# An attention and gated MLP kernel on one core: GpSimd clears, staggered prologue deadlines, and another split of exponentials between ScalarE and VectorE

## Chip, cores and metric

One core of a Trainium2 chip. The metric is the device time of one execution in microseconds (us), lower is better. Every run quoted here was in the fast state, with a granted TensorE clock of about 0.99.

## The reference

```python
xn = layernorm(x)                        # x: 1 x 2048 x 640, bf16
qkv = xn @ wqkv                          # 32 heads of 20
p = softmax(q k^T / sqrt(20));  s = (p v) @ wo
h  = gelu(layernorm(xn) @ w1)            # the side branch
x1 = xn + shift(h) @ w2                  # four column groups shifted by 1 or 2 rows
h2 = gelu(layernorm(x1) @ w3) @ w4       # 640 -> 1536 -> 640
out = x + s * silu(x1 + h2)
```

Softmax needs 32 x 2048 x 2048 exponentials. They are the bulk of the work.

## The kernel before

Heads are worked on four at a time: eight quads (0 to 7), each with four groups of 512 queries. A group has score tiles of 128 x 1024 in PSUM. ScalarE turns one into exponentials in one instruction (an "exp" below). Some tiles are taken in blocks by VectorE instead, which builds the exponential's bits with integer operations in several pieces; such a block takes two exps off ScalarE. The numbers in `ND` say how many blocks each group of each quad has.

The order of every engine is fixed when the kernel is built: the kernel carries a list scheduler with its own model of how long each operation takes, and `DUE` shifts the deadlines of the tasks. DMAs are issued from SyncE. `dlat` shifts the model's estimate of when a transfer lands.

```python
self.DUE = dict(k0=164.5, ..., v0=-37.7, v0s=0.02, ..., u7=-16.2, s7=52.2)
self.POOLN = [6, 7, 9, 12, 14]          # tiles normalised on GpSimd
self.TRA = [9, 11, 15, 19]              # transposes evicted by ScalarE
self.LAST = [[[4, 2], [7, 1]], [[6, 1]]]  # VectorE units in the two halves of the last group
self.ND = ([1,2,4,3], [2,3,3,4], [3,4,2,2], [3,2,4,4], [3,2,4,3], [4,3,4,3], [4,4,3,2], [4,4,3,0])
# ... cut ...
ms = pl.schedule(verbose=True)
```

The exponential, two PSUM banks (`hs`) in, one buffer of `PT` out:

```python
def exp_act(self, hs, sa):
    self.T("act", c_act(1024),
           lambda e: e.activation(self.PT[:, hp.slot, :], self.psum[:, 512*hs.slot:512*hs.slot+1024], AF.Exp, scale=cfg.scale),
           reads=[sa], writes=[pa], name=f"exp{self.step}", due=self.at(self.nact + 1), acq=("PT", hp), rel=hs)
```

After each group the sums go to DRAM and back, and their reciprocals once more, to be broadcast over partitions (cut to the second trip):

```python
T("sp", C_SP, lambda e: e.dma_start(dr[ob]..., RZ[:, ob, :]), reads=[A("RZ", ob)], writes=[("dr", ob)],
  is_dma=True, nbytes=8192, name=f"r0{quad}_{qc}", stream="r0", dlat=-840.0)
T("sp", C_SP, lambda e: e.dma_start(RB[:, :], bass.AP(dr.tensor, ...)), reads=[("dr", ob)], writes=[A("RB")],
  is_dma=True, nbytes=128 * 2048, name=f"r1{quad}_{qc}", stream="r1", dlat=3600.0)
```

The last group of quad 7 is worked in two halves of 256 queries; `LAST` gives the places and numbers of score tiles that VectorE takes there (each by itself, one exp fewer).

```python
for unit in at.get(x, []):
    for m, kx in enumerate(unit):
        hs, sa = scores(kx, "d")         # takes a score slot, like ScalarE's tiles
        T("dve", c_dve(1024), ...)       # first piece: reads PSUM, frees the slot
# ... cut: pieces from SBUF, then the sums on PE
```

Of the kernel before, what the change touches and what calls it, by code (L numbers as in the profile page):

```python
# [610 lines left out]
class Cfg:  # L611
# [5 lines left out]
    def __init__(self, S=2048, D=640, H=32, F=1536):  # L617
        self.S, self.D, self.H, self.F = S, D, H, F
        self.DH = D // H
        assert self.DH == 20 and D % 128 == 0 and F % 128 == 0 and S % 512 == 0  # L620
        self.NT = S // 128
        self.NQC = S // 512
        self.KC = D // 128
        self.FC = F // 128
        self.NQUAD = H // 4
        self.QW = 4 * self.DH
        self.scale = self.DH ** -0.5
        self.OFFSET = 60.0
        self.T0 = 38000.0
        self.STEP = 960.0  # L630
        self.DUE = dict(
            k0=164.5, k1=-174.5, k2=-113.6, k3=-166.6, k4=-173.8, v0=-37.7, v0s=0.02, v1=3.5, v1s=-17.41, w1=870.8,
            w1s=6.09, g1=108.7, x1=247.5, x1s=-10.34, wo=4.2, st=212.5, g3_0=333.3, g3_2=544.8, si_0=498.9, si_2=652.8,
            sis=10.98, u0=6.1, s0=-19.0, u1=82.8, s1=39.0, u2=-14.0, s2=-6.0, u3=-32.6, s3=24.8, u4=-8.0, s4=-2.3,
            u5=-17.0, s5=-15.1, u6=-44.4, s6=75.8, u7=-16.2, s7=52.2)
        self.BLK = [(2, 3), (6, 7), (10, 11), (14, 15)]
        self.RESERVE = 1000.0
        self.POOLN = [6, 7, 9, 12, 14]
        self.HPE = 0.0
        self.HDVE = 0.0  # L640
        self.THIRD = False
        self.FALL = False
        self.SAVE = 1
        self.AHEAD = 3
        self.UNITS = ((),
                      ((3, 0, 1),),
                      ((0, 0, 2), (2, 1, 2)),
                      ((0, 0, 2), (2, 1, 2), (7, 0, 1)),
                      ((0, 0, 2), (1, 1, 2), (3, 0, 2), (5, 1, 2)))
        self.HPS = 6  # L650
        self.FILL = 0
        self.LNA = [3, 4]
        self.TRA = [9, 11, 15, 19]
        self.ONP = 0
        self.LAST = [[[4, 2], [7, 1]], [[6, 1]]]
        self.ND = (
            [1, 2, 4, 3],
            [2, 3, 3, 4],
            [3, 4, 2, 2],
            [3, 2, 4, 4],  # L660
            [3, 2, 4, 3],
            [4, 3, 4, 3],
            [4, 4, 3, 2],
            [4, 4, 3, 0])
# [55 lines left out]
class Gen:  # L720
# [187 lines left out]
    def alloc_persistent(self):  # L908
        cfg = self.cfg
# [20 lines left out]
        T("dve", c_dve(4096, "4x"), lambda e: e.memset(self.QM[:, :, :, :], 0.0), writes=[A("QM", k) for k in range(2)], name="qm0", due=-40000.0)  # L930
# [18 lines left out]
        self.pl.pe_psum_atoms.update([("PV", 0), ("gate",)] + [("turn", k) for k in range(-9, 1024)])  # L949
# [4 lines left out]
        T("dve", c_dve(S, "4x"), lambda e: e.memset(self.KT[:, 1, :], 0.0), writes=[A("KT0")], name="kt0", due=-40000.0)  # L954
        T("dve", c_dve(S, "4x"), lambda e: e.memset(self.QT[:, 1, :], 0.0), writes=[A("QT0")], name="qt0", due=-40000.0)
# [160 lines left out]
    def prep(self):  # L1116
# [42 lines left out]
        for c in range(NQC):  # L1159
            at = [A("KT", 0, c)]  # L1160
            h, wa = self.mm_tile(f"KT_{c}", KC, 512, lambda k, j: Wp[:, 1, k, DH * j:DH * j + 32],
                                 lambda k, j, c=c: xnT[:, k, 512 * c:512 * c + 512], lambda k, c=c: [A("Wp", 1), A("xnT", k, c)], at)
            t1 = T("dve", c_dve(512), lambda e, h=h, c=c: e.tensor_reduce(MXc[:, c:c + 1], self.wbank(h)[:, 0:512], axis=AX.X, op=ALU.max,
                                                                         apply_absolute_value=True),
                   reads=[wa], writes=[A("MXc", c)], name=f"mx_{c}")
            T("act", c_act(512) + 100, lambda e, h=h, c=c: e.activation(KT[:, 0, 512 * c:512 * c + 512], self.wbank(h)[:, 0:512], AF.Identity,
                                                                        bias=self.eaug[:, 0:1], scale=mask[:, 0:1]),
              reads=[wa, A("eaug"), A("maskh"), A("MXc", c)], writes=at, name=f"kev_{c}", rel=h)
# [41 lines left out]
    def stack(self, st):  # L1210
# [14 lines left out]
        for qk, dst in ((1, self.dk), (0, self.dq)):  # L1225
            for c in range(NQC):
# [6 lines left out]
              writes=[("dkq", qk, st)], is_dma=True, nbytes=120 * 4096, name=f"dk{qk}_{st}", stream=f"dk{qk}", due=due)  # L1233
# [41 lines left out]
    def v_proj(self, hf):  # L1275
# [8 lines left out]
        T("pool", 1260, lambda e: e.memset(VA[:, :, :, :, 20:21], 1.0), writes=allv, name=f"VA1_{hf}")  # L1284
        T("pool", 1260, lambda e: e.memset(VA[:, :, :, :, 21:22], 0.0), writes=allv, name=f"VA0_{hf}")
        for n in range(cfg.NT):
            at = [A(f"VA{hf}", n)]
            h, wa = self.mm_tile(f"v{hf}_{n}", KC, HALF, lambda k, c, n=n: xnT[:, k, n * 128 + 32 * c: n * 128 + 32 * c + 32],
                                 lambda k, c: Wv[:, k, :], lambda k, n=n: [A("xnT", k, n // 4), A(f"Wv{hf}")], at)
# [71 lines left out]
    def last_half(self, quad, qc, half, gb):  # L1361
# [40 lines left out]
        for x, kt in enumerate(ks):  # L1402
# [9 lines left out]
            for unit in at.get(x, []):  # L1412
# [9 lines left out]
                for v in range(4):  # L1422
# [6 lines left out]
                    for m, kx in enumerate(unit):  # L1429
# [3 lines left out]
                          reads=[A("SS", k), A("VX") if not own else A(f"VA{hf}", kx), pva], name=f"pvd_h{half}_{kx}_{v}")  # L1433
# [245 lines left out]
    def wo_last(self, n, dst, dsta):  # L1679
# [11 lines left out]
        T("pe", c_pe(8, HALF), fn, reads=[A("On7", n // 2), A("Wo7")], writes=[sa], name=f"wob{n}", acq=("S", hs))  # L1691
# [262 lines left out]
```

## Time and profile before

| | before |
|---|---|
| time, median of 4 runs beside the changed kernel | 884.09 us (883.31 to 885.23) |
| span of the profiled run | 882.5 us |
| first exp starts / last exp ends | 40.69 / 868.39 us |
| exps on ScalarE | 828 |
| ScalarE idle between these two | 18.2 us |

The idle time in the last row is the sum of the gaps between the end of one ScalarE instruction and the start of the next. Loads of ScalarE's function table are counted as gap here, though `prof` counts them as busy: each of the three gelu rows has one before and one after it (2 x 1.28 us, 7.7 us in all). The lines behind the table are in the prediction. So the time has three parts: what precedes the first exp, the exps with the gaps between them, and what follows the last.

### The profile page before, as it was taken

Reading aid. Unit: us, or ns where it says so; the run is one execution under the profiler, and the core shown is the slowest. Engines: PE = TensorE matmul, PEld = TensorE weight load, DVE = VectorE, ACT = ScalarE, POOL = GpSimd, SP = SyncE. Lnnn points to the kernel's source line nnn. Section 1 sums busy time; section 2 is a strip of 40 time slices with the busy share of each in tenths; the row PEclk is TensorE's granted clock in tenths of the full one; section 3 lists DMA queues with packets and bytes.
Section 4 is the critical chain, followed back from the end, with each engine's and each line's share of the span. In section 5 each row is a group of like instructions: output and inputs, shape, how many; then the busy total and the mean of one; then the engine's idle time right before and its main releaser. Section 6 shows DMA issues by size and latency. Waiting matters only on the chain.

```text
span 882.5 us, 34883 instructions
## 1 busy us (share of the span) xinstructions
PE 827.6 (94%) x15958; PEld 370.6 (42%) x15958; DVE 730.4 (83%) x1005; ACT 838.6 (95%) x887; POOL 36.1 (4%) x71
## 2 busy tenths in 40 slices
PE   3999999999999999999998999999998899999996
PEld 2523333333444454343334445334333344533585
DVE  8747698587798989979998578998989787599976
ACT  5699999999999999999999999999999999999983
POOL 5500000000000000000000000000000000010000
PEclk9999999999999999999999999999999999999998
DMA  7002613431210002232323121321321212031332
GB/s 223 12 15 58 155 49 81 131 85 25 56 39 25 25 26 68 69 82 65 94 62 86 57 58 35 91 62 32 92 68 38 57 32 69 25 100 54 91 89 92
DMA packets 86482, 59.04 MB, mean 67 GB/s; under 512 B 53056, under 2 KB 77840, under 8 KB 86336
## 3 DMA queue, kind: packets, MB, share of 16 engines
q1 hardware_dynamic: 86336, 56.82, 23.7%
q8 instruction: 125, 2.05, 1.0%
q14 instruction: 21, 0.17, 0.1%
HBM read 42.10 MB, written 10.63 MB: 60 GB/s over the span
## 4 chain that ended last, share of the span: by engine, by line
ACT 66%; PE 25%; DVE 6%; DMA 2%; issue 1%; SPq 0%; DVEq 0%
ACT arena L1526 62%; PE psum L785 10%; PE psum L1502 7%; ACT arena L1896 2%; PE psum L1349 2%; PE psum L1484 2%; PE psum L1390 2%; PE psum L1476 2%; DMA queries<-arena 1%; ACT arena L1912 1%; DVE arena L1553 1%; DVE arena L1467 1%; DVE arena L988 1%; PE psum L1380 0%; DVE arena L1104 0%
## 5 line engine op out<-in xcount | busy, mean ns | idle before, releaser
L1526 ACT ACTIVATE arena<-psum 128x1024 bf16<-128x1024 f32 x828 | 771.7, 1038 | 11.0 <-PE psum L1390 3.3
L1502 PE MATMUL psum<-arena 128*32 128x512 bf16 x4640 | 353.2, 381 | 10.3 <-ACT arena L1526 8.5
L785 PE MATMUL psum<-arena 128*32 128x320 bf16 (+1 forms) x5952 | 356.7, 335 | 4.9 <-DVE arena L1291 1.6
L1553 DVE TENSOR_SCALAR arena<-psum 128x1024 uint16<-128x1024 f32 (+1 forms) x194 | 234.3, 1209 | 46.3 <-PE psum L1484 45.8
L1467 DVE TENSOR_SCALAR arena<-arena 128x4096 uint16<-128x4096 uint16 (+1 forms) x216 | 232.6, 1101 | 4.1 <-PE psum L1476 3.2
L785 PEld LDWEIGHTS psum<-arena 128*32 128x32 bf16 x5952 | 149.7, 97 | 135.2 <-issue 24.7
L1502 PEld LDWEIGHTS psum<-arena 128*32 128x32 bf16 x4640 | 97.6, 95 | 138.8 <-ACT arena L1526 104.2
L1349 PE MATMUL psum<-arena 128*22 128x512 bf16 x1600 | 152.3, 381 | 0.8 <-DVE arena L1588 0.4
L1476 PE MATMUL psum<-arena 128*22 128x512 bf16 x1536 | 124.5, 380 | 1.0 <-DVE arena L1467 0.9
L1484 PE MATMUL psum<-arena 32*128 32x512 bf16 x824 | 86.9, 387 | 12.1 <-ACT arena L1526 9.2
L1484 PEld LDWEIGHTS psum<-arena 32*128 32x128 bf16 x824 | 22.0, 91 | 102.3 <-ACT arena L1526 82.0
L1349 PEld LDWEIGHTS psum<-arena 128*22 128x22 bf16 x1600 | 39.9, 92 | 53.0 <-issue 12.7
L1476 PEld LDWEIGHTS psum<-arena 128*22 128x22 bf16 x1536 | 36.8, 92 | 42.3 <-DVE arena L1467 7.4
L1230 DVE CAST arena<-psum 128x512 bf16<-128x512 f32 x40 | 27.4, 687 | 16.5 <-PE psum L785 16.4
L1892 DVE CAST arena<-psum 128x512 bf16<-128x512 f32 x48 | 32.9, 685 | 6.6 <-PE psum L785 6.6
L1907 DVE TENSOR_TENSOR arena<-psum,arena 128x320 bf16<-128x320 f32 x32 | 15.6, 487 | 12.2 <-PE psum L785 11.9
L1676 DVE SCALAR_TENSOR_TENSOR arena<-psum,arena 128x320 bf16<-128x320 f32 x32 | 15.6, 487 | 10.2 <-PE psum L785 10.2
L1821 DVE TENSOR_TENSOR arena<-psum,arena 128x512 bf16<-128x512 f32 x20 | 13.8, 688 | 10.6 <-PE psum L785 10.6
L1094 PE MATMUL psum<-arena 128*32 128x128 bf16 x320 | 8.6, 245 | 14.2 <-DVE arena L1003 12.8
L988 DVE BATCH_NORM_STATS2 arena<-arena 128x6 f32<-128x320 bf16 x50 | 21.7, 477 | 0.1
L1601 DVE TENSOR_TENSOR arena<-arena 128x512 bf16<-128x512 f32 x28 | 19.1, 683 | 3.1 <-DMA arena<-recips 3.1
L1588 DVE COPY arena<-psum 128x512 f32<-128x512 f32 x28 | 19.2, 685 | 2.4 <-PE psum L1349 1.4
(116 smaller groups left out, 337.3 us busy)
## 6 DMA issues: line engine op xcount, KB each, us to landing
arena<-in_B_w_dram SPq DMA_DIRECT2D x48, 160.0 KB, 2.6
arena<-recips SPq DMA_DIRECT2D x28, 256.0 KB
arena<-arena SPq DMA_DIRECT2D x124, 32.0 KB, 1.9
arena<-in_B_w_dram SPq DMA_DIRECT2D x4, 960.0 KB, 5.6
arena<-in_A_x_dram SPq DMA_DIRECT2D x8, 320.0 KB, 5.7
arena<-in_A_x_dram SPq DMA_DIRECT2D x16, 160.0 KB, 2.7
out_dram<-arena SPq DMA_DIRECT2D x16, 160.0 KB, 2.1
arena<-keys SPq DMA_DIRECT2D x28, 80.0 KB
```

What stands on the lines that cost most here:

```text
L785: ins = e.matmul(pb[32 * c:32 * c + 32, 0:N], lhsT(k, c), rhs(k, c), start=(k == 0), stop=(stop and k == nk - 1), tile_position=(0, 32 * c))
L988: lambda e, li=li, n=n, hh=hh: e.bn_stats(st[:, li, 6 * hh:6 * hh + 6], xn[:, n, hD * hh:hD * hh + hD]),
L1230: T("dve", c_dve(512), lambda e, h=h, c=c: e.tensor_copy(KS[:, 512 * c:512 * c + 512], self.wbank(h)[:, 0:512]), reads=[wa], writes=[A("KS ...
L1349: ins = e.matmul(pb[32 * i:32 * i + 22, 0:512], VA[:, ql, kts[i // 2], i, :], PT[:, slots[i // 2][0].slot, 512 * (i % 2):512 * (i % 2) + 512],
L1467: T("dve", c_dve(w, "4x"), lambda e, v=v, dst=dst: e.tensor_scalar(dst, U[:, ub, 0:w], 0.5, EXP_B[v], op0=ALU.mult, op1=ALU.add), reads=ha ...
L1476: ins = e.matmul(pb[32 * i:32 * i + 22, 0:512], wv, dst[:, at:at + 512].bitcast(BF16), start=first, stop=final, tile_position=(0, 32 * i))
L1484: return e.matmul(out, self.KT[32 * i:32 * i + 32, b, 128 * kt:128 * kt + 128], self.QT[32 * i:32 * i + 32, b, 512 * qc:512 * qc + 512], s ...
L1502: ins = e.matmul(out[32 * c:32 * c + 32, :], self.KT[:, b, 128 * kt + 32 * c:128 * kt + 32 * c + 32], self.QM[:, gb, 2 * a + jj, :], start ...
L1526: lambda e: e.activation(self.PT[:, hp.slot, :], self.psum[:, 512 * hs.slot:512 * hs.slot + 1024], AF.Exp, scale=cfg.scale),
L1553: ins = e.tensor_scalar(U[:, ub, 1024 * at + 512 * k:1024 * at + 512 * k + w], self.psum[:, 512 * hd.slots[k]:512 * hd.slots[k] + w], a_ex ...
L1588: T("dve", c_dve(512), lambda e: e.tensor_copy(Ob[:, :], self.bank(self.PVB)[:, :]), writes=[("PV", 0), A("Ob")], name=f"ob{quad}_{qc}", c ...
L1892: T("dve", c_dve(512), lambda e, h=h, fc=fc, i=i: e.tensor_copy(GT[:, i, fc, :], self.wbank(h)[:, 0:512]), reads=[wa], writes=at, name=f"g ...
```

## The change

Its intent: start the exps earlier, give ScalarE fewer of them in the middle, and shorten the tail. The core of the diff:

```diff
-  k0=164.5, ..., v0=-37.7, v0s=0.02, ...
+  k0=267.2, ..., v0=-19.2, v0s=-1.11, ..., mx=-20.5, mxs=19.19     # nearly all deadlines differ
-  self.POOLN = [6, 7, 9, 12, 14]
+  self.POOLN = [0, 14]
-  self.TRA = [9, 11, 15, 19]
+  self.TRA = [0, 2, 3, 4, 6, 8, 9, 11, 15, 17, 18]
-  self.LAST = [[[4, 2], [7, 1]], [[6, 1]]]
+  self.LAST = [[[0, 2], [7, 1]], [[1, 1], [2, 1]]]
-  [1,2,4,3], [2,3,3,4], [3,4,2,2], [3,2,4,4], [3,2,4,3], [4,3,4,3], [4,4,3,2], [4,4,3,0]
+  [1,3,4,3], [2,3,4,4], [3,4,2,2], [4,2,4,4], [3,3,4,2], [3,3,4,3], [4,4,3,4], [4,2,2,3]
-  T("dve", c_dve(4096, "4x"), lambda e: e.memset(self.QM...    # and two clears of 2048
+  T("pool", 3500, lambda e: e.memset(self.QM...
   # V tiles from number 6 on come after the last key tile:
+  ..., [("ktp",)] if n >= cfg.VAFTER else [])
-  writes=[("dkq", qk, st)], is_dma=True, nbytes=120 * 4096, name=f"dk{qk}_{st}"
+  writes=[("dkq", qk, st)], is_dma=True, nbytes=120 * 4096, dlat=1200.0, name=f"dk{qk}_{st}"
   # sums of the last half go ahead of the output projection:
+  name=f"pvd_h{half}_{kx}_{v}", cls=-half
```

(The fourth number of quad 7 in `ND` is not used; `LAST` holds in its place.)

More of the change, by code (lines that the diff above doesn't have):

```diff
@@ L631, in __init__ @@
         self.DUE = dict(
-            k0=164.5, k1=-174.5, k2=-113.6, k3=-166.6, k4=-173.8, v0=-37.7, v0s=0.02, v1=3.5, v1s=-17.41, w1=870.8,
-            w1s=6.09, g1=108.7, x1=247.5, x1s=-10.34, wo=4.2, st=212.5, g3_0=333.3, g3_2=544.8, si_0=498.9, si_2=652.8,
-            sis=10.98, u0=6.1, s0=-19.0, u1=82.8, s1=39.0, u2=-14.0, s2=-6.0, u3=-32.6, s3=24.8, u4=-8.0, s4=-2.3,
-            u5=-17.0, s5=-15.1, u6=-44.4, s6=75.8, u7=-16.2, s7=52.2)
+            k0=267.2, k1=-160.8, k2=-134.1, k3=-147.5, k4=-77.1, v0=-19.2, v0s=-1.11, v1=106.4, v1s=-21.98, w1=681.5,
+            w1s=2.58, g1=146.2, x1=275.3, x1s=-14.58, wo=-37.3, st=210.6, g3_0=308.2, g3_2=540.8, si_0=584.9, si_2=663.7,
+            sis=-0.73, u0=4.9, s0=-16.9, u1=76.3, s1=29.1, u2=-36.3, s2=50.1, u3=-50.5, s3=69.1, u4=-23.0, s4=17.0,
+            u5=-31.9, s5=-17.5, u6=-14.3, s6=7.6, u7=-39.5, s7=70.1, mx=-20.5, mxs=19.19)
         self.BLK = [(2, 3), (6, 7), (10, 11), (14, 15)]
-        self.RESERVE = 1000.0
-        self.POOLN = [6, 7, 9, 12, 14]
+        self.RESERVE = 0.0
+        self.POOLN = [0, 14]
         self.HPE = 0.0
@@ L651, in __init__ @@
         self.FILL = 0
-        self.LNA = [3, 4]
-        self.TRA = [9, 11, 15, 19]
+        self.LNA = [3, 3]
+        self.VAFTER = 6
+        self.TRA = [0, 2, 3, 4, 6, 8, 9, 11, 15, 17, 18]
         self.ONP = 0
-        self.LAST = [[[4, 2], [7, 1]], [[6, 1]]]
+        self.LAST = [[[0, 2], [7, 1]], [[1, 1], [2, 1]]]
         self.ND = (
-            [1, 2, 4, 3],
-            [2, 3, 3, 4],
+            [1, 3, 4, 3],
+            [2, 3, 4, 4],
             [3, 4, 2, 2],
-            [3, 2, 4, 4],
-            [3, 2, 4, 3],
-            [4, 3, 4, 3],
-            [4, 4, 3, 2],
-            [4, 4, 3, 0])
+            [4, 2, 4, 4],
+            [3, 3, 4, 2],
+            [3, 3, 4, 3],
+            [4, 4, 3, 4],
+            [4, 2, 2, 3])
     def order(self, quad, qc):
@@ L929, in alloc_persistent @@
         self.QM = self.alloc("QM", [2, 4, 512], BF16)
-        T("dve", c_dve(4096, "4x"), lambda e: e.memset(self.QM[:, :, :, :], 0.0), writes=[A("QM", k) for k in range(2)], name="qm0", due=-40000.0)
+        T("pool", 3500, lambda e: e.memset(self.QM[:, :, :, :], 0.0), writes=[A("QM", k) for k in range(2)], name="qm0", due=-40000.0)
         self.U = self.alloc("U", [2, 4096], U16)
@@ L948, in alloc_persistent @@
             self.pl.pe_psum_atoms.add(("S", b))
-        self.pl.pe_psum_atoms.update([("PV", 0), ("gate",)] + [("turn", k) for k in range(-9, 1024)])
+        self.pl.pe_psum_atoms.update([("PV", 0), ("wob",), ("ktp",), ("gate",)] + [("turn", k) for k in range(-9, 1024)])
         self.PVB = 7
@@ L953, in alloc_persistent @@
         self.grp = 0
-        T("dve", c_dve(S, "4x"), lambda e: e.memset(self.KT[:, 1, :], 0.0), writes=[A("KT0")], name="kt0", due=-40000.0)
-        T("dve", c_dve(S, "4x"), lambda e: e.memset(self.QT[:, 1, :], 0.0), writes=[A("QT0")], name="qt0", due=-40000.0)
+        T("pool", 1800, lambda e: e.memset(self.KT[:, 1, :], 0.0), writes=[A("KT0")], name="kt0", due=self.at(10))
+        T("pool", 2150, lambda e: e.memset(self.QT[:, 1, :], 0.0), writes=[A("QT0")], name="qt0", due=self.at(12))
         T("dve", c_dve(S, "4x"), lambda e: e.tensor_scalar(self.KT[:, 1, :], self.KT[:, 1, :], self.eaug[:, 0:1], None, op0=ALU.add),
@@ L1160, in prep @@
             at = [A("KT", 0, c)]
+            last = [("ktp",)] if c == NQC - 1 else []
             h, wa = self.mm_tile(f"KT_{c}", KC, 512, lambda k, j: Wp[:, 1, k, DH * j:DH * j + 32],
-                                 lambda k, j, c=c: xnT[:, k, 512 * c:512 * c + 512], lambda k, c=c: [A("Wp", 1), A("xnT", k, c)], at)
+                                 lambda k, j, c=c: xnT[:, k, 512 * c:512 * c + 512], lambda k, c=c: [A("Wp", 1), A("xnT", k, c)], at + last)
             t1 = T("dve", c_dve(512), lambda e, h=h, c=c: e.tensor_reduce(MXc[:, c:c + 1], self.wbank(h)[:, 0:512], axis=AX.X, op=ALU.max,
                                                                          apply_absolute_value=True),
-                   reads=[wa], writes=[A("MXc", c)], name=f"mx_{c}")
+                   reads=[wa], writes=[A("MXc", c)], name=f"mx_{c}", due=self.at(0, "mx", 1, "mxs", c))
             T("act", c_act(512) + 100, lambda e, h=h, c=c: e.activation(KT[:, 0, 512 * c:512 * c + 512], self.wbank(h)[:, 0:512], AF.Identity,
@@ L1232, in stack @@
             T("sp", C_SP, lambda e, dst=dst: e.dma_start(dst[DH * h0:DH * (h0 + nh), :], KS[0:DH * nh, :]), reads=ksa,
-              writes=[("dkq", qk, st)], is_dma=True, nbytes=120 * 4096, name=f"dk{qk}_{st}", stream=f"dk{qk}", due=due)
+              writes=[("dkq", qk, st)], is_dma=True, nbytes=120 * 4096, dlat=1200.0, name=f"dk{qk}_{st}", stream=f"dk{qk}", due=due)
             if qk == 1:
@@ L1283, in v_proj @@
         allv = [A(f"VA{hf}", n) for n in range(cfg.NT)]
-        T("pool", 1260, lambda e: e.memset(VA[:, :, :, :, 20:21], 1.0), writes=allv, name=f"VA1_{hf}")
-        T("pool", 1260, lambda e: e.memset(VA[:, :, :, :, 21:22], 0.0), writes=allv, name=f"VA0_{hf}")
+        T("pool", 1260, lambda e: e.memset(VA[:, :, :, :, 20:21], 1.0), writes=allv, name=f"VA1_{hf}", due=None if hf == 0 else self.at(250))
+        T("pool", 1260, lambda e: e.memset(VA[:, :, :, :, 21:22], 0.0), writes=allv, name=f"VA0_{hf}", due=None if hf == 0 else self.at(250))
         for n in range(cfg.NT):
@@ L1288, in v_proj @@
             h, wa = self.mm_tile(f"v{hf}_{n}", KC, HALF, lambda k, c, n=n: xnT[:, k, n * 128 + 32 * c: n * 128 + 32 * c + 32],
-                                 lambda k, c: Wv[:, k, :], lambda k, n=n: [A("xnT", k, n // 4), A(f"Wv{hf}")], at)
+                                 lambda k, c: Wv[:, k, :], lambda k, n=n: [A("xnT", k, n // 4), A(f"Wv{hf}")], at, [("ktp",)] if n >= cfg.VAFTER else [])
             T("dve", c_dve(HALF),
@@ L1432, in last_half @@
                                                  lambda i, k=k, m=m: SS[:, k, 1024 * m + 256 * i:1024 * m + 256 * i + 256].bitcast(BF16)),
-                          reads=[A("SS", k), A("VX") if not own else A(f"VA{hf}", kx), pva], name=f"pvd_h{half}_{kx}_{v}")
+                          reads=[A("SS", k), A("VX") if not own else A(f"VA{hf}", kx), pva], name=f"pvd_h{half}_{kx}_{v}", cls=-half)
             T("pe", c_pe(4, 256), pv(vown, kt, lambda i, hp=hp: PT[:, hp.slot, 256 * i:256 * i + 256]), reads=[pa, A(f"VA{hf}", kt), pva], rel=hp,
@@ L1690, in fn @@
             return ins
-        T("pe", c_pe(8, HALF), fn, reads=[A("On7", n // 2), A("Wo7")], writes=[sa], name=f"wob{n}", acq=("S", hs))
+        T("pe", c_pe(8, HALF), fn, reads=[A("On7", n // 2), A("Wo7")], writes=[sa, ("wob",)], name=f"wob{n}", acq=("S", hs))
         def fe(e):
```

## The prediction

> **What bounds the kernel now.** I read the page's busy shares and slices first, then the busy time by stage, then the ordered rows of each engine at both ends.
>
> ```profile
> PE 827.6 (94%) x15958; PEld 370.6 (42%) x15958; DVE 730.4 (83%) x1005; ACT 838.6 (95%) x887; POOL 36.1 (4%) x71
> ACT  5699999999999999999999999999999999999983
> L1526 ACT ACTIVATE arena<-psum 128x1024 bf16<-128x1024 f32 x828 | 771.7, 1038 | 11.0 <-PE psum L1390 3.3
> ```
>
> ScalarE is 95% busy, nearly all of it in 828 exponentials (line 1526). A row lasts 1.04 us, but 78 of them in a row took 72.37 us, so each advances the clock by 0.93 us. ScalarE is short of work only in the first two slices and the last two. So the kernel is a prologue, a long stretch bound by ScalarE, and a tail. The busy times by stage (start:end, length, then PE, weight loads, VectorE, ScalarE, GpSimd) say the same:
>
> ```profile
> 0.00:20.00 20.00, 6.52 (x150) 4.45 (x154) 17.08 (x48) 10.07 (x23) 10.50 (x36) 1.00 0.81 247
> 20.00:40.70 20.70, 19.12 (x580) 11.97 (x572) 17.25 (x52) 11.36 (x20) 13.11 (x15) 1.00 0.05 11
> 360.00:465.00 105.00, 102.27 (x1800) 40.31 (x1796) 93.29 (x122) 104.39 (x113) 1.45 (x3) 1.00 0.29 72
> 675.00:780.00 105.00, 98.42 (x1940) 45.61 (x1932) 79.71 (x93) 103.67 (x101) 0.01 (x1) 0.98 0.16 45
> 835.00:868.40 33.40, 33.40 (x1080) 26.81 (x1076) 23.91 (x48) 29.86 (x32) 0.00 (x0) 1.00 0.27 80
> 868.40:882.50 14.10, 6.16 (x160) 4.67 (x150) 9.95 (x22) 0.00 (x0) 0.00 (x0) 0.78 0.32 106
> ```
>
> In the middle ScalarE is at 99%, even where VectorE is at 93.29 of 105. In the last 33 us before the last exponential PE has no gap and ScalarE has 3.5 us of them. After it come 14.1 us without any ScalarE work.
>
> The prologue (first exponential at 40.69):
>
> ```profile
> 1.30 1.76 DVE L930 MEMSET arena<- 128x2048 uint32 x1 [1.30 <-PEq L1939]
> 13.49 1.44 DVE L1003 TENSOR_SCALAR arena<-arena 128x640 bf16<-128x640 bf16 x1
> 13.50 1.25 POOL L1285 MEMSET arena<- 128x256 bf16 x1
> ...
> 16.63 4.35 PE L785 MATMUL psum<-arena 128*32 128x320 bf16 x80
> 20.95 0.92 ACT L1045 ACTIVATE arena<-arena 128x640 bf16<-128x640 bf16 x1 [5.78 <-DVE arena L1036]
> 40.69 7.44 ACT L1526 ACTIVATE arena<-psum 128x1024 bf16<-128x1024 f32 x8 [0.61 <-PE psum L1484]
> ```
>
> From 16.63 PE does four V tiles, and VectorE, in order behind their evictions, issues the small line-1036 operation only at 20.77, though GpSimd's power before it was done at 18.08. ScalarE stands 5.78 us for it. The same recurs at 30.62 (4.32 us). So V work, which no exponential needs yet, stands ahead of the norm chain, which every exponential needs. In all 252 of the 128x320 V matmuls, 12.6 tiles of 20, ran before 40.7.
>
> The tail:
>
> ```profile
> 868.67 3.47 PE L785 MATMUL psum<-arena 128*32 128x320 bf16 x96
> 871.93 0.76 PE L1688 MATMUL psum<-arena 128*32 128x320 bf16 x16
> 872.47 0.54 PE L1380 MATMUL psum<-arena 128*22 128x256 bf16 x12
> 877.00 1.26 PE L1688 MATMUL psum<-arena 128*32 128x320 bf16 x16 [2.92 <-DVE arena L1450]
> ```
>
> The last half-tile's sums (line 1380) wait behind 96 output-projection matmuls. VectorE's last piece then waits for a buffer until 873.32, and everything that ends the kernel follows it.
>
> **What the Trainium skill says.** (1) "Perfetto Trace Analysis", Identifying the Most-Contended Engine: occupancy is fair for ScalarE and VectorE, not for matmuls. The trace agrees: PE at 94% feeds ScalarE with 99% in the middle. I treat PE as the bound only where ScalarE waits for it, in the last 33 us. (2) "VectorE: DVE Perf Modes", Zero memsets can be issued as uint32: one cycle per element, at four bytes. The 128x1024 uint32 clears start 1.08 us before what follows, which is 1024/0.96 GHz. (3) "SBUF — State Buffer", Who interferes with whom: a GpSimd operation and a two-port VectorE operation exclude each other for a whole instruction. The trace fits: the norm at 13.49 took 1.44 us instead of some 0.4, and ended as GpSimd's clear did (14.75). (4) "GPSIMD Engine Reference", Engine selection: one-input operations run about at line rate. Only half so here: a 128x640 norm took 0.88 us on GpSimd as multiply-add, but 2.50 us as subtract-multiply, against 0.35 to 0.48 on VectorE.
>
> **The change, part by part.**
>
> Prologue, PE. V tiles from number 6 on must follow the last key tile, so 6 precede it and perhaps one or two fill gaps after it, instead of 12.6. That is about 6 fewer at 0.77 us (40 matmuls took 1.54): 4.6 us off an engine that is busy 25.6 of the 28.5 us from its start at 12.18 to 40.69.
>
> Prologue, VectorE. The clears (1.76 + 0.91 + 0.91) go to GpSimd and the 1.16 us addition moves behind a late deadline. They ran mostly before the input was there, so I count only the 0.6 us by which statistics begin late (6.81 against ScalarE's 6.17). Seven more transposes leave for ScalarE (4 to 11): 7 x 0.35 = 2.4. Six V evictions: 6 x 0.41 = 2.5. One more tile's statistics come in (2 x 0.40 + 0.10 = 0.9), and one more norm (8 to 9: 0.36). Net: 4.2 us less.
>
> Prologue, ScalarE. 7 x 0.49 = 3.4 of evictions come in. One tile's two sums leave (2 x 0.86 = 1.7); two more norms come (3 to 5: 2 x 0.83 = 1.7). Net: 3.4 more, into 19 us of idle time. GpSimd gets the 4096-element clear, two of 2048, and tile 0's norm, and loses four norms; it was idle from 6.3 to 10.5 and more.
>
> The first exponential needs all sixteen tiles, so it follows the packed work of PE and VectorE, which shrinks by 4.2 to 4.6, plus part of the two norm waits (2.7 and 2.1 us lost between power and line 1036). Against that stands tile 0's slower norm at the head (2.50 instead of 0.4) and its lock. I choose **-5 us**: first exponential near 35.7.
>
> Middle (quads 0 to 6). The count of VectorE blocks goes from 85 to 89. Each takes two exponentials off ScalarE: 8 x 0.93 = **-7.4 us**. A block costs VectorE about 2 x 1.13 + 4 x 0.57 = 4.5 us. The most heavily changed quad is 6 (13 to 15): its window goes from 79.7 in 105 to about 88.8 in 101, 88%, under the 89% of the quad at 360 to 465 that keeps ScalarE at 99%. The V tiles put off return inside quad 0, where PE has 5 us free of 104: I add **+1.5 us** of waits. The deadlines of the side branch only move filler, and its gelu and silu rows are unchanged.
>
> Quad 7. Its first three groups go from 11 blocks to 8, and the split last group from 4 units to 5: 6 - 1 = 5 more exponentials, 4.7 us. PE pays more too: by start-to-start spacings, two key tiles on ScalarE cost 4 x 0.43 + 2 x 0.22 = 2.16 us, a block 2 x 0.33 + 5 x 0.22 = 1.76. So 3 x 0.4 + 0.3 = 1.5 us. From 780 to 868.4 ScalarE was busy 84.5 of 88.4 and PE 85.5, so part disappears in those gaps: **+2.5 us**.
>
> Tail. The last half's VectorE sums get a class above the output projection, and its units start at positions 1 and 2 instead of 6. The buffer wait until 873.32 should go. The projection's 3.5 us of matmuls and their evictions remain, though beside the closing chain: **-3 us**.
>
> Sum: -5 - 7.4 + 1.5 + 2.5 - 3 = -11.4, so 883.7 - 11.4 = 872.3; I write **872.5 us**.
>
> **Rivals.** (A) The prologue is held elsewhere: tile 0's norm of 2.5 us on GpSimd starts PE later than 12.18, and its lock stops VectorE's norms; or ScalarE's in-order evictions become the new wait. For it: the locked 1.44 us norm, and a stretch of 5.78 us in which ScalarE blocked itself. Against: six V tiles off PE are real work gone. Then the prologue gives 1 to 2 us, and the time is 876 to 877. (B) PE becomes the bound when fuller: V tiles in quad 0 and the projection in quad 7 leave ScalarE waiting, and the gain in exponentials is given back. For: the 33.40 of 33.40. Against: the middle's 99%. Time: about 878. (C) All works better: the prologue packs to near 33 us (VectorE's remaining work is about 23 us from 6.2 by the durations above, so 31 with some waits) and the tail falls to 9 us: 866 to 868. (D) The new order brings late transfers or VectorE lag in quads 3 and 6: +3 to +10, so 876 to 883.
>
> **Range and chances.** The four terms have spreads of about 2.5, 2.5, 2 and 2 us, together some 4.5 and, with the unknown reordering, 5. That makes 866 to 879 an 8-in-10 range. Faster by over 2% means below 866.0, at (C)'s edge: 0.11. Slower by over 2% would need a broken schedule: 0.02. Within 2%: 0.87.
>
> **What would show it.** Right: first exponential between 34 and 38 us; about 8 V tiles before it; no 5 us ScalarE wait for line 1036's successor; 825 exponentials at an unchanged spacing of 0.93; ScalarE 98% or more in quads 0 to 6; under 12 us after the last exponential, with line 1380's sums ahead of the projection. Wrong: a first PE transpose after 14 us with a late first exponential (A); ScalarE waits on PE of over 3 us more in quad 0 or 7 (B); waits for line 1553 or VectorE pieces in quad 6 (D).

## The result

The changed kernel took 888.64 us (median of 4 runs, 887.12 to 889.21) beside 884.09 us. Ratios in this document are the mean time of one kernel's fast runs over the mean of the other's fast runs of the same rounds, so they are not quite the ratio of the quoted medians. Here it is 1.0048, with a 95% interval of 1.003 to 1.0065. It is slower by half a per cent, where 1.3% faster was predicted.

The page of the changed kernel: busy shares, ScalarE's slices, and the group of exps.

```profile
PE 829.2 (93%) x15958; PEld 371.5 (42%) x15958; DVE 735.0 (83%) x1007; ACT 840.6 (95%) x889; POOL 41.9 (5%) x73
ACT  6799799999999999999999999999989999999985
L1528 ACT ACTIVATE arena<-psum 128x1024 bf16<-128x1024 f32 x825 | 769.9, 1038 | 27.1 <-PE psum L1504 10.0
```

Both ends of the slices are better and there are three exps fewer, as planned. But the idle time before the exps went from 11.0 to 27.1 us. A slice of 22 us with 90% or more shows as 9, so the row of digits hides most of this.

The busy time by quad shows where. First the kernel before in quads 0, 5, 7 and the tail (start:end, length, then busy time of PE, weight loads, VectorE, ScalarE, GpSimd, and clock, DMA share, GB/s):

```profile
40.69:143.50 102.81, 97.77 (x1522) 34.94 (x1522) 74.64 (x90) 100.68 (x108) 1.39 (x3) 0.98 0.28 71
560.80:656.10 95.30, 93.34 (x1720) 38.89 (x1712) 87.28 (x100) 95.26 (x103) 0.00 (x0) 1.00 0.26 64
767.30:868.39 101.09, 97.59 (x2272) 53.27 (x2268) 90.21 (x126) 97.21 (x105) 3.07 (x3) 1.00 0.28 80
868.39:882.50 14.11, 6.17 (x160) 4.68 (x150) 9.96 (x22) 0.00 (x1) 0.00 (x0) 0.78 0.32 106
```

The same for the changed kernel:

```profile
37.89:145.40 107.51, 101.15 (x1610) 37.39 (x1610) 81.02 (x101) 99.16 (x107) 3.13 (x8) 0.98 0.26 71
559.20:661.70 102.50, 97.31 (x1736) 39.74 (x1724) 84.45 (x101) 97.76 (x106) 0.00 (x0) 0.98 0.26 63
767.90:879.05 111.15, 106.80 (x2583) 61.51 (x2572) 88.44 (x131) 103.26 (x111) 2.94 (x3) 1.00 0.27 79
879.05:887.50 8.45, 1.29 (x28) 0.56 (x28) 5.55 (x12) 0.00 (x1) 0.00 (x0) 0.78 0.28 97
```

In quad 0 ScalarE has 1.5 us less to do and takes 4.7 us longer. In quad 5 ScalarE is idle for 102.50 - 97.76 = 4.74 us, where before it was idle for 0.04. Quad 7 is 10 us longer with 6 us more ScalarE work, and the tail is 5.6 us shorter. By parts:

| us | before | after | after - before | predicted |
|---|---|---|---|---|
| up to the first exp | 40.7 | 37.9 | -2.8 | -5 |
| quads 0 to 6 | 726.6 | 730.0 | +3.4 | -5.9 |
| quad 7 | 101.1 | 111.1 | +10.0 | +2.5 |
| tail | 14.1 | 8.5 | -5.6 | -3 |
| span | 882.5 | 887.5 | +5.0 | -11.4 |

And ScalarE's gaps by quad:

| us | q0 | q1 | q2 | q3 | q4 | q5 | q6 | q7 | sum |
|---|---|---|---|---|---|---|---|---|---|
| before | 2.1 | 4.3 | 0.5 | 0.5 | 3.0 | 0.0 | 3.9 | 3.9 | 18.2 |
| after | 8.4 | 3.0 | 1.9 | 3.8 | 0.2 | 4.7 | 3.6 | 7.9 | 33.4 |

In quads 3 and 4 most of the difference is one gelu row with its two table loads, which starts at 465.65 us before (in quad 4) and at 444.73 us after (in quad 3): 2.6 us of gap that moved.

The prologue of the changed kernel answers to the waits of 5.78 us and 4.32 us that were shown of before. PE's first row, ScalarE's longest wait, and the first exps:

```profile
12.05 1.04 PE L1095 MATMUL psum<-arena 128*32 128x128 bf16 x32 [12.05 <-POOL arena L1004]
22.48 1.08 ACT L1102 ACTIVATE arena<-psum 128x512 bf16<-128x512 bf16 x2 [2.23 <-PE psum L1095]
37.89 2.85 ACT L1528 ACTIVATE arena<-psum 128x1024 bf16<-128x1024 f32 x3 [1.57 <-PE psum L1486]
```

The long waits are gone and PE starts no later than before (12.18), although it waits for GpSimd's norm of tile 0. In the tail, the last half's sums (line 1382 now) come right after their exps, and only the closing chain is left:

```profile
879.11 0.29 PE L1382 MATMUL psum<-arena 128*22 128x256 bf16 x4 [0.35 <-ACT arena L1528]
879.22 0.45 PE L1690 MATMUL psum<-arena 128*32 128x320 bf16 x8
882.31 0.73 PE L1690 MATMUL psum<-arena 128*32 128x320 bf16 x16 [2.64 <-DVE arena L1452]
```

**What held ScalarE in quad 0.** Its rows there, in the changed kernel:

```profile
90.69 2.85 ACT L1528 ACTIVATE arena<-psum 128x1024 bf16<-128x1024 f32 x3 [1.70 <-PE psum L1504]
94.69 1.94 ACT L1528 ACTIVATE arena<-psum 128x1024 bf16<-128x1024 f32 x2 [1.14 <-PE psum L1486]
97.98 1.94 ACT L1528 ACTIVATE arena<-psum 128x1024 bf16<-128x1024 f32 x2 [1.36 <-PE psum L1486]
```

The scores were late because PE, in order, stood before another matmul, and that one waited for a DMA:

```profile
89.59 0.62 PE L786 MATMUL psum<-arena 128*32 128x512 bf16 x8 [1.55 <-DMA keys<-arena]
```

The write-out of keys (line 1234) was issued at 83.14 us, though its data had been ready at about 80.5. The waits of the issuing queue between 78 and 86 us tell why:

```profile
SPq L1599 <- DVE arena L1597: 5.6, 1, 5.6
SPq L1601 <- DMA recips<-arena: 2.3, 1, 2.3
```

Line 1601, the broadcast read of the reciprocals, stood at the head of the queue for 2.3 us until their write had landed. Issues are in order, so the ready key write-out stood behind it. The 8 KB write took 3.6 us to land here; the median of the 28 is 1.5:

```profile
DMA to landing us min/median/max: 1.4/1.5/3.6
```

Slow landings also occur in the kernel before: 4 of its 28 took 3.4 to 3.9 us. The scheduler's model puts this write 0.84 us earlier than its plain estimate (`dlat=-840.0` above). In quad 5 it is the same picture with a weight load: the load of a W3 part stood behind such a read for 2.7 us, PE waited 2.85 us for it, and ScalarE 2.96:

```profile
651.57 1.02 ACT L1528 ACTIVATE arena<-psum 128x1024 bf16<-128x1024 f32 x1 [2.96 <-PE psum L1504]
```

### The profile page after: what moved, and what is told of

Its sections match the earlier page's. It is cut to its first block, busy times and chain, and to the rows that moved or that the text cites. A ratio compares the mean times of both kernels' runs of the same rounds, so it can differ in the third digit from the quotient of the medians.

```text
span 887.5 us, 34865 instructions
## 1 busy us (share of the span) xinstructions
PE 829.2 (93%) x15958; PEld 371.5 (42%) x15958; DVE 735.0 (83%) x1007; ACT 840.6 (95%) x889; POOL 41.9 (5%) x73
## 4 chain that ended last, share of the span: by engine, by line
ACT 60%; PE 28%; DVE 8%; DMA 4%; issue 0%; SPq 0%; DVEq 0%
ACT arena L1528 55%; PE psum L786 11%; PE psum L1504 8%; PE psum L1351 3%; PE psum L1486 3%; ACT arena L1898 2%; DVE arena L1555 2%; DVE arena L1469 2%; PE psum L1478 2%; PE psum L1392 1%; ACT arena L1827 1%; DMA arena<-sums 1%; DMA arena<-in_A_x_dram 1%; DMA arena<-in_B_w_dram 1%; DMA rstd<-arena 1%; DMA sums<-arena 1%
## 5 line engine op out<-in xcount | busy, mean ns | idle before, releaser
L1528 ACT ACTIVATE arena<-psum 128x1024 bf16<-128x1024 f32 x825 | 769.9, 1038 | 27.1 <-PE psum L1504 10.0
L1469 DVE TENSOR_SCALAR arena<-arena 128x4096 uint16<-128x4096 uint16 (+1 forms) x216 | 235.1, 1110 | 3.2 <-PE psum L1478 1.9
L1351 PE MATMUL psum<-arena 128*22 128x512 bf16 x1596 | 152.0, 380 | 0.6 <-DVE arena L1590 0.4
L1478 PE MATMUL psum<-arena 128*22 128x512 bf16 x1552 | 128.3, 381 | 2.9 <-DVE arena L1469 2.6
L1293 DVE CAST arena<-psum 128x320 bf16<-128x320 f32 x32 | 15.1, 484 | 7.2 <-PE psum L786 6.9
```

Of the source, the lines that this page charges most:

```text
L1351: ins = e.matmul(pb[32 * i:32 * i + 22, 0:512], VA[:, ql, kts[i // 2], i, :], PT[:, slots[i // 2][0].slot, 512 * (i % 2):512 * (i % 2) + 512],
L1469: T("dve", c_dve(w, "4x"), lambda e, v=v, dst=dst: e.tensor_scalar(dst, U[:, ub, 0:w], 0.5, EXP_B[v], op0=ALU.mult, op1=ALU.add), reads=ha ...
L1478: ins = e.matmul(pb[32 * i:32 * i + 22, 0:512], wv, dst[:, at:at + 512].bitcast(BF16), start=first, stop=final, tile_position=(0, 32 * i))
```

## The experiments

Three questions were open. **Queue:** do the two stalls come from the order in the issuing queue (T1), and are they all of the loss in quads 0 to 6? **Quad 7:** is what the tail gains just paid for in quad 7, and do its gaps come from PE, from VectorE's order or from the score slots? **Prologue:** is the earlier first exp a real gain, or a loan that quad 0 pays back because the V tiles still have to be done (T4)?

Undoing a parameter of the scheduler reshuffles all the orders behind it. So, wherever possible, the experiments kept the built order ("pinned") and changed one thing after scheduling.

### after_spswap: two swaps in the issuing queue

```diff
     ms = pl.schedule(verbose=True)
+    # in SyncE's order only: the waiting read goes behind the ready transfers
+    for late, early in (("r10_0", ["dk1_0", "rr0"]), ("r15_2", ["ld_w3_3_6"])):
+        ...rotate their places...
```

> The changed kernel with the same order on every compute engine; only two places of the DMA issue order differ: the key write-out and the write of the reciprocal standard deviations of quad 0 go ahead of the broadcast read of the first softmax reciprocals, and one W3 load of quad 5 goes ahead of another such read. Theory T1 (the changed order lets PE wait on transfers that stand in the issue queue behind a read which itself waits for a DMA to land, and ScalarE starves behind PE): the waits near exponentials 54 to 63 (about 4.7 us of slip against the schedule) shrink to under 2 us and those near exponentials 610 to 614 (4.6 us) vanish, so 887.5 of span becomes 879 to 882. Rival T2 (the four added VectorE blocks of quads 0 to 6 load VectorE or PE beyond what they can give, wherever the transfers stand): less than 1.5 us of gain.

Measured: correct, 879.12 us (878.64 to 880.7), before 883.58 there; ratio 0.9951 (0.9938 to 0.9963). The span fell from 887.5 to 879.0. Gaps in quad 0 went from 8.4 to 3.6 us and in quad 5 from 4.7 to 0.4. ScalarE's rows, where the stalls had been:

```profile
84.71 6.67 ACT L1538 ACTIVATE arena<-psum 128x1024 bf16<-128x1024 f32 x7
91.89 5.94 ACT L1538 ACTIVATE arena<-psum 128x1024 bf16<-128x1024 f32 x6 [0.51 <-PE psum L1496]
```

```profile
644.12 11.38 ACT L1538 ACTIVATE arena<-psum 128x1024 bf16<-128x1024 f32 x12
```

So it is shown that the place behind the waiting reads made the stalls: three transfers moved past two such reads are worth 8.5 us of span. The place cost time in two ways. The transfers were issued later, and once issued, right behind the 256 KB read, they also landed more slowly: the key write-out in 6.4 us instead of 4.1, the W3 part in 5.5 instead of 2.4. Counted from the issue of the write that the read waits for, the keys landed 5.0 us earlier after the swap, of which 2.6 us are the earlier issue; the W3 part 4.9 us earlier, of which 1.9. No run separates the two.

Quads 0 to 6 now take 721.6 us (37.5 to 759.1), 5.0 less than before. That is close to the -5.9 predicted, but not quite for its reasons: 1.2 us of it is a silu row that moved to quad 7, and the gaps are still 3.4 us longer than before (17.8 against 14.3), not 1.5. This version beats both kernels.

### before_q7: the kernel before with the new quad 7

```diff
-  [4, 4, 3, 0])
+  [4, 2, 2, 0])
   # plus LAST and the class of the last half's sums, as in the changed kernel
```

> The kernel before with quad 7 alone as in the change: 8 blocks for 11 in its first three groups, 5 units for 4 in its last group, and the last sums in the higher class; the order of all engines is that of the kernel before up to 789 us of the schedule. Prediction's sum: +2.5 of exponentials -3 of tail = -0.5 us. Theory T3 (quad 7 and the tail are bound by PE, whose work is nearly the same; exponentials added there fill gaps and the tail shrinks by what they push forward): last exponential later by 5 to 7 us, tail shorter by as much, total within 1.5 us of before. Rival: the five exponentials cost their 4.7 us in full, as the comparison of the two traces from the start of quad 7 suggests (+4.4 us).

Measured: correct, 883.04 us (882.35 to 884.39), ratio 0.9996 (0.9983 to 1.001). Quad 7 took 106.4 us instead of 101.1, and the tail 9.2 instead of 14.1. The sum is +0.4 us: in this order the tail's gain is paid for in quad 7.

### after_q7old: the changed kernel with the old quad 7

```diff
-  [4, 2, 2, 3])
+  [4, 4, 3, 3])
   # plus LAST and the class, as in the kernel before
```

> The changed kernel with quad 7 alone as before (11 blocks, 4 units, lower class); same order on every engine up to 787 us of the schedule. T3: total within 2 us of the changed kernel, or some 3 us slower as the kernel's own schedule has it. Rival (quad 7 with fewer VectorE blocks costs 4.4 us): 4 us faster than the changed kernel.

Measured: correct, 890.13 us (888.14 to 893.15), ratio 1.0075 (1.0059 to 1.0091). With five exps fewer quad 7 took 114.7 us, with 16.0 us of gaps, and the tail stayed at 8.4. So the rival (4 us faster with the old blocks) is wrong. But 8.8 of the 16.0 us are one gap at 822 us, in which PE, by its order, does some 210 matmuls of the output projection before the sums that free a buffer for the next exp. The run tells of this schedule, then, and not of what VectorE can keep up with. The stalls in quads 0 and 5 were there as in the changed kernel.

### before_prologue: the new prologue alone

```diff
+  # LNA, TRA, POOLN and the clears as in the changed kernel; its order up to the first exp,
+  # then the order of the kernel before, both by a table of priorities
```

> The kernel before with the prologue alone as in the change (the same engines for norms, transposes and clears, the same order up to the first exponential), and after it the order of the kernel before; blocks and tail as before. Prediction's step: first exponential earlier and the whole kernel with it, -3 us or more. Theory T4 (PE is full from its first transpose at 12.1 us to the end of quad 0, so an earlier first exponential is borrowed from work that PE then does under the exponentials): first exponential near 38 us instead of 40.7, but exponential 60 at the old time and the total within 1 us of before.

Measured: correct, 881.4 us (879.89 to 882.1), ratio 0.9972 (0.9959 to 0.9984). The first exp came at 37.4 us (41.2 in before_q7, which has the old prologue), quad 0 took 103.9 instead of 102.8 us, and everything after kept the lead: the last exp ended at 866.3 (868.4). So some 1 us is paid back in quad 0 and 2.2 to 2.5 us are kept. The loan theory is wrong for the larger part; the step's own "-3 us or more" was not reached either.

### after_r1pool and before_r1pool: the waiting reads on another queue

```diff
+  # after scheduling: all 28 reads r1 leave SyncE's order and enter GpSimd's by planned start
+  t.eng = "pool"
```

> The changed kernel with all orders kept, except that the 28 broadcast reads of the softmax reciprocals (each waits for its own write to land) are issued from GpSimd's queue, so that nothing stands behind them on the sync queue. T1 (head-of-line waits in the issue queue): the waits of quads 0 and 5 go as with the two moved places, 879 to 882 us, perhaps a little better because every such place is covered. Rival T5 (it was those transfers' order on the wires, not the waiting queue head): no gain. A cost that may hide it: a read issued by GpSimd may land later than one issued by sync, which shows as waits of the multiply after it.

> The same move in the kernel before. T1: the kernel before had no damaging place (its slip against the schedule grew by under 2 us in the whole middle), so it gains 0 to 1.5 us; the difference between the two kernels turns from +5 to -3 us. T5: no change in either.

Measured: after_r1pool 885.54 us (883.68 to 886.5), before 883.96 there, ratio 1.0017 (1.0003 to 1.0032). before_r1pool 884.03 us, ratio 1.0009 (0.9989 to 1.003). The 879 to 882 us expected of the first were not reached. In the changed kernel both stalls went again (gaps in quad 0 4.2, in quad 5 0.4), without the swaps. As the key write-out and the W3 part were again issued ahead of the read, the rival T5 is not excluded by it. But a new one came in quad 1, where VectorE and then ScalarE waited for such a read:

```profile
165.27 0.69 DVE L1611 TENSOR_TENSOR arena<-arena 128x512 bf16<-128x512 f32 x1 [6.10 <-DMA arena<-recips]
```

```profile
168.57 1.02 ACT L1536 ACTIVATE arena<-psum 128x1024 bf16<-128x1024 f32 x1 [3.77 <-PE psum L1512]
```

The page's DMA issues give the time from issue to landing for a read issued by GpSimd, 5.4 us in the median:

```profile
arena<-recips POOLq DMA_DIRECT2D x28, 256.0 KB, 5.4
```

The one that VectorE waited for took 9.2 us, with six reads of `rstd` from SyncE issued within 4 us of it. No figure for the same read from SyncE is in the profile, but VectorE waited 6.5 us for these reads in all here, against 2.4 us in the changed kernel (8.3 against 3.1 in the pair of before). So the second queue took the stalls away and VectorE's waits grew; why those reads landed late was not tested.

### spswap_light and before_light: a void test

```diff
-                for c in range(4):
+                for c in (range(4) if not light or k in (0, nk - 1) else (3,)):
```

(in the output projection, quad 7 and tail; wrong result, relative error 0.617)

> Wrong result on purpose: the changed kernel with the moved DMA places, and of the output projection in quad 7 only the first and last of its 5 or 6 terms in full, the others with one of their four column matmuls; all orders kept. It takes some 10 us of work off PE in quad 7. T3 (quad 7 is bound by PE, so more exponentials there fill its gaps and work shifted there costs): ScalarE's gaps in quad 7 fall from 7.9 us to under 3 and the total by 5 us or more against the run with the moved places (879.1). Rival (quad 7 is bound by ScalarE, or by latencies between engines): less than 2 us.

> Wrong result on purpose: the same lightening of the projection in the kernel before. T3: its quad 7 has 3.9 us of ScalarE gaps and 3.5 us of projection after the last exponential, so it gains 4 to 7 us. Rival: less than 2 us in quad 7, and at most 2.5 us in the tail.

Measured: 880.53 us (ratio 0.9964) and 883.25 us (0.999). Quad 7 of spswap_light took 111.1 us with 7.9 us of gaps, as without the edit. PE had 360 fewer matmuls of 2580 in it, but was busy for 106.75 us instead of 106.79. The four matmuls of a set go to four column groups and run side by side, so leaving out three of four freed nothing. The Trainium skill says that such matmuls run concurrently, in "TensorE: Matmul & The Clock Gate", Part 3: Packing small matmuls; the trace agrees, with 0.04 us. The test says nothing on PE.

### spswap_narrow and before_narrow: PE made lighter

```diff
+                w = 32 if light and 0 < k < nk - 1 else N
-                    ins = e.matmul(pb[32 * c:32 * c + 32, 0:N], lhsT(k, c), rhs(k, c), ...
+                    ins = e.matmul(pb[32 * c:32 * c + 32, 0:w], lhsT(k, c), rhs(k, c)[:, 0:w], ...
```

> Wrong result on purpose. The kernel with the two queue swaps, same order on every engine, but in the output projection (all of it in quad 7 and the tail) the middle k steps of each tile move 32 columns instead of 320: some 112 sets of four matmuls, each about 0.1 us shorter (a set of 320 columns takes 0.15), so some 10 us of PE's 106.8 us in quad 7 go. This is the lightening that the void test was to be. Theory PE (quad 7 is 96% busy on PE, and ScalarE's 7.9 us of gaps there are PE's lack of time): gaps in quad 7 fall below 4 us, the quad from 111.1 to 107 or less, and the time from 879.1 to about 874.5. Rival VectorE (the gaps come from PE and ScalarE waiting for buffers that VectorE frees late): gaps stay above 6.5 us and the time at 878 to 879.5.

> Wrong result on purpose. The kernel before with the same narrowing of the projection's middle k steps. Control: in the kernel before, quad 7 has 3.9 us of gaps and PE 97.6 us busy of 101.1, so both theories allow little: theory PE says 1 to 2.5 us come off (gaps to about 2), rival VectorE says none (883 to 884.5). If it gains as much as the run with the swaps, the lack of PE time is not what the change brought.

Measured (wrong, 0.676): 879.4 us (878.48 to 880.33), before 884.9 there, ratio 0.9949 (0.9925 to 0.9973); and 883.46 us, ratio 0.9988 (0.9959 to 1.0017). Quad 7 of spswap_narrow:

```profile
759.00:870.00 111.00, 103.21 (x2588) 55.74 (x2584) 88.53 (x132) 103.41 (x111) 2.94 (x3) 1.00 0.27 80
```

The quad itself runs from 759.50 to 870.16 (110.7 us). PE lost 3.6 us of busy time in the window (4.1 between the quad's own ends), not the 10 that I had estimated, because narrow sets are not that much shorter: 480 matmuls of 32 columns were busy for 13.4 us, 496 of 320 columns for 27.6. But ScalarE's gaps are the same seven gaps, 7.6 us against 7.9. Theory PE expected less than 4. With PE now idle for 7.8 us of the 111, all seven gaps kept nearly their size (the longest went from 2.19 to 1.95 us), so PE's load as a whole is not what sets them. A larger relief was not tried.

### spswap_gshort: VectorE's long products made shorter

```diff
-  e.scalar_tensor_tensor(xn[:, n-1:n+1, :], TH[:, :, :], 1.0, xn[:, n-1:n+1, :], ...      # 1.48 us
+  e.scalar_tensor_tensor(xn[:, n-1:n+1, 0:160], TH[:, :, 0:160], 1.0, ...                 # 0.48 us, quad 7 only
```

> Wrong result on purpose. The kernel with the two queue swaps, same order, but the three closing products of the side branch in quad 7 (the 1.48 us VectorE operation ahead of which buffer releases stood) work on 160 instead of 640 columns of each of two tiles, some 0.4 us each: 3.2 us of VectorE work fewer, at just the places where ScalarE's gaps of 1.75 and 0.73 us were traced to them. Rival VectorE: these gaps go, quad 7's gaps fall from 7.9 to 5.5 or less, and the time to about 876.5. Theory PE: PE, which has no slack, takes the wait elsewhere; gaps in the quad stay above 6.8 us and the time above 878.

Measured (wrong, 0.297): 879.4 us (878.9 to 879.95), ratio 0.9949 (0.9926 to 0.9972). The two gaps that I had put down to these products stayed: after_spswap, then spswap_gshort, first of the two.

```profile
768.82 1.02 ACT L1538 ACTIVATE arena<-psum 128x1024 bf16<-128x1024 f32 x1 [1.75 <-PE psum L1361]
```

```profile
767.28 1.02 ACT L1538 ACTIVATE arena<-psum 128x1024 bf16<-128x1024 f32 x1 [1.61 <-PE psum L1361]
```

The second gap was 0.73 us in both. So the length of these products isn't it either. The first gap lies where quad 6 hands over to quad 7: the sums of the new quad can start only when the single accumulator of the old one has been copied out, and in spswap_gshort that copy itself waited 0.59 us for PE. This is read from the trace, not tested.

### spswap_nolast: no VectorE units in the last group

Five of the seven gaps, 5.1 us, lie in the split last group. There each VectorE unit takes one of the score slots for the 1.22 us of its first piece. A score tile fills two banks of PSUM, and the kernel gives scores four banks, so there are two slots. In spswap_narrow, where PE has time to spare, the row after two such units in a row shows PE waiting for the slot:

```profile
839.89 0.62 PE L1515 MATMUL psum<-arena 128*32 128x512 bf16 x8 [0.21 <-DVE arena L1432]
```

```diff
-  self.LAST = [[[0, 2], [7, 1]], [[1, 1], [2, 1]]]
+  self.LAST = [[], []]
```

> The kernel with the two queue swaps, without any VectorE units in the split last group (LAST = [[], []]): 830 exponentials instead of 825; the order up to about 820 us is unchanged. Theory slots (the score tiles have two slots, and each unit that VectorE takes holds one for 1.2 us, two units both: the five gaps of 0.6 to 2.2 us, 5.1 us together, from 840 to 860 us are the price of the five units): those gaps fall to under 1.5 us in all, five exponentials bring 4.7 us, and the time stays at 878.5 to 880. Rival PE (quad 7 simply has too much PE work, so gaps are taken elsewhere): gaps stay above 5 us and the time rises by 3 us or more, to 882.

Measured: correct, 878.78 us (875.86 to 879.23), before 884.83 there, ratio 0.9927 (0.9911 to 0.9944). ScalarE's rows from 834 us on, in the kernel before:

```profile
833.70 7.44 ACT L1526 ACTIVATE arena<-psum 128x1024 bf16<-128x1024 f32 x8
842.92 3.07 ACT L1526 ACTIVATE arena<-psum 128x1024 bf16<-128x1024 f32 x3 [1.79 <-PE psum L1390]
846.72 11.27 ACT L1526 ACTIVATE arena<-psum 128x1024 bf16<-128x1024 f32 x12 [0.72 <-PE psum L1390]
858.73 9.66 ACT L1526 ACTIVATE arena<-psum 128x1024 bf16<-128x1024 f32 x10 [0.74 <-PE psum L1390]
```

and in spswap_nolast:

```profile
833.13 34.30 ACT L1538 ACTIVATE arena<-psum 128x1024 bf16<-128x1024 f32 x37
```

The kernel before has a gap for each place in `LAST` (4 units at 3 places, 3.3 us). Without units there is none: 37 exps in a row at 0.927 us. Quad 7 has five exps more and is 1.5 us shorter (109.7 against 111.1 to 111.2); its gaps are 2.6 us. So it is shown that the units make these gaps: a unit saves an exp of 0.93 us and costs a wait of 0.8 us (3.3 for 4, before) to 1.0 us (5.1 for 5). That they do it through the slots is read from the PE row above, not shown by this run, which took away their work on VectorE and PE as well. The tail stayed short (9.3 us), so its gain doesn't depend on the units. It is the best version that I ran. Whether it beats after_spswap, which ran in other rounds, is not settled: their intervals touch.

### replanned and replanned3: schedules searched with late transfers

```diff
-  stream="r0", dlat=-840.0      |  dlat=1200.0, name=f"dk...   |  T("act", 2750 + ...   # gelu
+  stream="r0", dlat=700.0       |  dlat=2200.0, name=f"dk...   |  T("act", 4150 + ...
+  self.DUE, self.ND, self.POOLN, self.LNA, self.TRA, self.LAST = ...found by search...
```

> A version to beat both: the changed kernel with its deadlines, block counts and prologue lists searched anew (5,300 trials of its own scheduler), with three durations in the scheduler's model of time made late on purpose: the write of the reciprocals lands 1.5 us later, the key write-out 1 us later, the gelu row takes the table load[...]. Theory late transfers (the loss came of schedules tuned so tightly against a model in which transfers are early that one late landing is passed on): no ScalarE wait in quads 0 to 6 that the schedule does not have already, spread between runs below 3 us, and a time of 872 to 879. Rival (the model is not the reason; any densely tuned order loses 5 to 10 us on the chip): gaps of over 15 us in quads 0 to 6 and 883 or more.

> As replanned, from another start and another seed of the search (planned 1.7 us longer). Theory late transfers: 873 to 881, gaps in quads 0 to 6 within 4 us of the schedule's own. Rival: 884 or more.

Measured: both correct; 882.88 us (881.59 to 886.85), ratio 0.9987 (0.9967 to 1.0007), and 881.82 us (880.6 to 883.57), ratio 0.9972 (0.9958 to 0.9987). No quad of replanned took over 0.9 us more than its schedule said, and none of replanned3 over 0.5: the unplanned stalls are gone. (The schedules' times come from building the kernels; they are in no profile.) But the times expected, 872 to 879 and 873 to 881, were not reached, the runs of replanned spread over 5.3 us and not under 3, and its gaps in quads 0 to 6 were 26.4 us (18.7 without the table loads), over the 15 that the rival named, though the schedule had them already. A schedule that has room for late transfers everywhere had no surprise and no great speed. The two swaps did better than replanned; the intervals of after_spswap and replanned3, from different rounds, overlap a little.

## Why the prediction was wrong

- **Prologue, "-5 us".** It was -2.8 in the profiled pair, and -2.2 to -2.5 in before_prologue. The mechanism was right: the two long waits are gone. The size was off, first in the V term: 184 of the 128x320 matmuls, 9.2 tiles, ran before the first exp (252, 12.6 tiles, before). So 3.4 tiles left, not 6: at 0.77 us 2.6 us instead of 4.6. The "about 6" did not even fit the "about 8 V tiles before it" of the same prediction, which makes 4.6 tiles and 3.5 us. In all PE was busy for 3.8 us less before the first exp (21.80 against 25.64), but idle for 1.0 us more. Another 1 us comes back in quad 0. Rival (A) was wrong on PE's start: it came at 12.05.
- **Middle, "-7.4" of exps.** Right: 8 exps fewer in quads 0 to 6. The page's 825 in all were foreseen too.
- **Middle, "+1.5 us of waits".** This is the step that failed most. The gaps of quads 0 to 6 grew by 11.2 us (25.5 against 14.3), not 1.5, so these quads went +3.4, not -5.9 us. I put the waits down to the V tiles on PE in quad 0. I had rival (D), "late transfers", but expected them in quads 3 and 6 and read no wait of the issuing queue. after_spswap shows what they were: two reads that waited for a write to land held up ready transfers, in quads 0 and 5. That cost 8.5 us of span. With them out of the way, quads 0 to 6 are at -5.0.
- **Quad 7, "+2.5", and tail, "-3".** They came to +10.0 and -5.6. In quad 7 "part disappears in those gaps" is the second step that failed: the five exps cost their 4.7 us in full, and the gaps grew, by 4.0 us. The five VectorE units of the last group cost 5.1 us (four cost 3.3 before), and the handover from quad 6 and one more wait came to 2.5. One silu row of 1.2 us moved into quad 7 as well. The tail gained more than I thought because the projection's line 786 left it altogether (28 matmuls remain, against 160). In the order of the kernel before, my sum of -0.5 was about right: before_q7 shows +0.4 in the spans and a ratio of 0.9996.
- **PE as the bound of quad 7, rival (B).** PE is 96% busy there, but making it 3.6 us lighter left the gaps at 7.6 us (7.9). The occupancy was no evidence, as "Perfetto Trace Analysis", Identifying the Most-Contended Engine, quoted in the prediction, warns. In quad 0 the sign named for (B) did come (gaps 8.4 against 2.1), but behind PE stood a DMA.
- **One reading.** The locked norm at 13.49 ended at 14.93, so 0.18 us after GpSimd's clear and not with it; no later step rests on this.

What stays open: the 2.5 us of waits early in quad 7, and the rest of the gaps in quads 0 to 6 that the swaps left (3.4 us more than before); no run took them apart.

## What to carry to other kernels

In a kernel with fixed orders, a DMA that waits for its data holds every transfer behind it in the same issuing queue: read the queue's own waits, and put those that wait for another transfer's landing behind those that are ready. A block that is moved from a full engine to one with time pays only if it doesn't hold the buffer that the full engine needs next; here a VectorE unit cost ScalarE about as much as it saved. And after a denser schedule, compare the idle time before the main instruction, not the shares: 95% stayed 95% while 15 us were lost.

## What the Trainium skill lacked or had wrong

- "DMA: Bandwidth & Descriptors", Issuing engines are not separate DMA queues, says that issuing from several engines only saves the time to initiate a DMA. The runs show more: a DMA that waits for its semaphore holds up those behind it in its engine's stream (2.3 and 2.7 us here), and two such places cost 8.5 us of span. Moving the waiting reads to another engine's queue took both stalls away, though not the loss (885.54 us).
- No page has a figure for how much later a transfer lands that is issued right behind another: behind the 256 KB broadcast read the key write-out took 6.4 us to land and a W3 part 5.5, ahead of it 4.1 and 2.4.
- No page has the spread of small writes as a distribution: an 8 KB write to DRAM landed in 1.5 us in the median and up to 3.6 us, in the kernel before up to 3.9.
- "DMA: Bandwidth & Descriptors", Specifications, gives first-byte latencies of about 1 us for GpSimd's DMAs and 0.6 for sync's. No run here measures a first byte, so none contradicts this; what the page lacks is the time of a broadcast read as a whole. Those of 256 KB issued by GpSimd took 5.4 us to land in the median and up to 9.2.
- "TensorE: Matmul & The Clock Gate", Part 3, was right on column groups side by side: 360 matmuls fewer freed 0.04 us of 106.79.
